# Attention and gated MLP on one core: products of a job under way go ahead of a due batch of values, and unread products behind the jobs that stand in the last layernorm

## The chip, the cores and the metric

The kernel runs on one core of a Trainium2 chip. The metric is the device time of one execution in microseconds (us); lower is better. The engines are TensorE (PE: matmuls; PEld: its weight loads), VectorE (DVE), ScalarE (ACT), GpSimd (POOL) and SyncE (SP, which only issues DMAs here). Each takes its instructions in the order in which the program has them; between engines, semaphores make one wait for another.

## The reference, cut to what matters

One sequence of 2048 rows of 640 values; 32 heads of 20 values each; a gated layer of 1728 columns. All arrays are bfloat16.

```python
def _layernorm(x, axis=-1, eps=1e-5):
    m = jnp.mean(x, axis=axis, keepdims=True)
    v = jnp.var(x, axis=axis, keepdims=True)
    return (x - m) / jnp.sqrt(v + eps)

def _A_ref(x, wqkv, wo):
    q, k, v = ...            # (x @ wqkv), split into 32 heads of 20
    scores = jnp.einsum("bhqd,bhkd->bhqk", q, k) * (Dh ** -0.5)
    p = _softmax(scores, axis=-1)
    o = jnp.einsum("bhqk,bhkd->bhqd", p, v)
    return ... @ wo

def _B_ref(x, w_gate, w_up, w_down):
    g = jnp.einsum("bsd,df->bsf", x, w_gate)
    u = jnp.einsum("bsd,df->bsf", x, w_up)
    return jnp.einsum("bsf,fd->bsd", g * u, w_down)

h = x + _A_ref(_layernorm(x, axis=-1), A_wqkv, A_wo)
h2 = h + _B_ref(_layernorm(h, axis=-1), B_w_gate, B_w_up, B_w_down)
```

## The kernel before, in words

**Scores and exponentials.** The softmax needs one exponential for each of 32 x 2048 x 2048 scores. They are made in 683 *score tiles* of 128 partitions (keys) by 1536 columns (queries). For each tile `emit_S` puts the score products on TensorE (L533; they use 32 of the 128 rows of the array) and one ACTIVATE on ScalarE (L547), which writes a tile E. For some tiles ScalarE does only the first 1024 columns: the last third is computed by VectorE with four instructions (`emit_x` and what follows it, L580 to L591; tiles xv, xt, xe). `x_takes` decides that while the program is written: VectorE must be free in time, and in the last quarter of the queries `room()` must find that the jobs still to do leave enough time.

**Values.** `emit_AV` (L740) multiplies E with the values and adds up in the one PSUM bank acc, in batches of two rounds; these products too are small ones (the rows of four heads side by side). The ones column in the values gives the softmax sums. When a segment (four heads, 512 or 256 queries) is complete, VectorE copies acc (L752).

**Jobs.** All other work of TensorE is cut into jobs that run between score tiles: transposes of normalised rows, projections of q, k and v (L303, L317), and for each quarter of the queries the product with wo (`job_out`, L978), the second layernorm's transposes, the gated layer (`job_glu`, L1065 and L1083: the products with w_up, "wu", and w_gate, "wg", then h = g * u) and the down product (`job_y`, L1129, evacuated by VectorE at L1133, stored by SP at L1139). The weights wu and wg come through two buffers each, or lie in the places of the old queries ("qa"). A job makes one chunk after another; all jobs but few share the one PSUM bank mi, which VectorE has to empty between two chains of products.

**What sets the order.** The Python code is also a planner. It keeps clocks of its own (`at["pe"]`, `at["dve"]`, `at["exp"]`, `at["slot"]`) with assumed durations, and for each score tile i it writes one *slot*, in this order: the score products of tile i and its exponential; then up to two batches of values, if they are due; then finished segments and new jobs; then products of jobs (`run_job`), as many as by the planner's clock end before the next score products have to start; then, if nothing fits, `keep_warm` (L496): a pair of *unread products*, matmuls of ident with kT whose result nobody reads. `cool` lets `emit_S` put a single unread product (L529) ahead of the scores where too few full-array products stood of late. A job that is not at the start of a chain (`cur["fresh"]` is false) has its bank already. The due times in `run_job(until)` come from the next exponential and from the release of the score tile two before.

**The end.** When the last values are through, jobs are taken until none is in the middle of a chain, and `last_tail` does the last 256 queries: out products (L1228, L1230, L1234), with the last softmax sums and their reciprocals between them (L670, L678 to L686, L1243), the second layernorm (bn statistics, then rows normalised half on VectorE, L1257, and half on ScalarE, L1258), then `fill()`, then the transposes of the normalised rows (L283), the gated layer and y. `fill()` does all jobs that are left; at that point these are half tiles of y (14 products each) of the quarter's first 256 queries. By program order they stand between the out products and the transposes.

Behind all this stands a general branch that a flag skips.

Of the kernel before, what the change touches and what calls it, by code (L numbers as in the profile page):

```python
# [61 lines left out]
WO_NS, SUMS_NS, ROOT_NS, ROWS_NS = 1500, 6000, 5000, 5000  # L62
END_OF_TIME = 10 ** 9
WARM_LATE, NEXT_DVE = 0, 300
HOLD_AT, HOLD_NS = 5300, 450
AV_ROUNDS, X_LATE = 2, 0
FULL_IN, FULL_NS, ALL_NS = 2083, 300, 760
# [18 lines left out]
def kernel(  # L86
# [617 lines left out]

    final = {}

    def emit_AV(upto):
        put_x()
        if not av_q:
            return  # L710
        if acc["seg"] is not None and av_q[0][1] != acc["seg"]:
            need_x(acc["seg"])
            put_x()
        s = av_q[0][1]
        p, g, lo, hi, kind = segs[s]
        b, c0, w = PASS[p]
        if acc["seg"] != s:
            if at["pe"] < at["acc"] and now["i"] < acc["from"] and min(u[0] for u in av_q) > now["i"] - E_BUFS:
                return
            acc["seg"], acc["left"], acc["n"] = s, (hi - lo) * HPG, [0] * HPG  # L720
            acc["t"] = accp.tile([P, QB], F32, name="acc")
        most, rows = AV_ROUNDS * HPG * QB // w, [[] for _ in range(HPG)]
        for u in av_q:
            if u[0] > upto or u[1] != s:
                break
            if len(rows[u[3]]) < most // HPG:
                rows[u[3]].append(u)
        ready = sum(len(r) for r in rows)
        if ready < min(most, acc["left"]) and min(u[0] for u in av_q) > upto - E_BUFS + 3:
            return  # L730
        for u in [r[k] for k in range(most // HPG) for r in rows if k < len(r)]:
            av_q.remove(u)
            _, _, kt, j, e = u
            x_used.add((s, kt, j))
            at["pe"] = max(at["pe"], x_ready.get((s, kt, j), 0))
            while x_live and x_live[0] in x_used:
                x_live.popleft()
            ensure(("v", kt, g // (NG // 2)))
            h = HPG * g + j
            nc.tensor.matmul(  # L740
                acc["t"][SLOT * j:SLOT * (j + 1), 0:w],
                lhsT=vx[kt][:, VS * h:VS * h + SLOT], rhs=e,
                start=(acc["n"][j] == 0), stop=(acc["n"][j] == hi - lo - 1))
            acc["n"][j] += 1
        acc["left"] -= ready
        partly.append((at["pe"], ready * w / 9.6))
        at["pe"], at["mode"] = pe_free("A") + -(-ready // HPG) * (w * 5 // 12 + 4), "A"
        if acc["left"] == 0:
            dve(605 if w == QB else 342, 0)
            if kind in ("copy", "only"):  # L750
                asb = parts[g] if kind == "copy" else nrm.tile([P, QB], F32, name="asb")
                nc.vector.tensor_copy(asb[:, 0:w], acc["t"][:, 0:w])  # L752
                if kind == "copy":
                    part[g] = asb
            else:
                asb = part[g]
                nc.vector.tensor_tensor(asb[:, 0:w], acc["t"][:, 0:w], asb[:, 0:w], ALU.add)
            acc["seg"], acc["from"], at["acc"] = None, now["i"] + 2, at["dend"] + DVE_PE
            if s == FINAL:
                final["asb"] = asb  # L760
            elif (p, g) in FAST:
                opens["nf", p, g] = at["dend"] + DVE_PE
                urgent.append((("nf", p, g), job_norm(s, asb)))
            elif kind in ("only", "last"):
                norm(s, asb)
# [448 lines left out]
    def run(gen):  # L1214
        for _ in gen:
            pass

    def last_tail():
        st = tail_st[LAST_B]
        on = On  # L1220
        asb = final["asb"]
        c0 = LAST_T[0] * P
        ps_h = {}

        def out_most(t, hf):
            ps = ps_h[t, hf] = bank()
            cs = slice(hf * HALF, (hf + 1) * HALF)
            nc.tensor.matmul(ps[:, 0:HALF], lhsT=ident[:], rhs=st["xr"][t][:, cs], start=True, stop=False)  # L1228
            for g in range(NG - 1):
                nc.tensor.matmul(ps[:, 0:HALF], lhsT=on[g][:, t * P:(t + 1) * P], rhs=wo[g][:, cs], start=False, stop=False)  # L1230

        def out_last(t):
            for hf in range(2):
                nc.tensor.matmul(ps_h[t, hf][:, 0:HALF], lhsT=on[NG - 1][:, t * P:(t + 1) * P],  # L1234
                                 rhs=wo[NG - 1][:, hf * HALF:(hf + 1) * HALF], start=False, stop=True)
        ta, tb = LAST_T
        out_most(ta, 0)
        bc = sums_to_rows(sums_on_pe(asb, HW), HW)
        out_most(ta, 1)
        ps = rows_to_cols(bc, HW, accp.tile([P, QB], F32, name="acc"))  # L1240
        for k in range(2):
            cs = slice(k * P, (k + 1) * P)
            nc.vector.tensor_tensor(on[NG - 1][:, c0 + k * P:c0 + (k + 1) * P], asb[:, cs], ps[:, cs], ALU.mult)  # L1243
        out_most(tb, 0)
        out_last(ta)
        out_most(tb, 1)
        out_last(tb)
        mv = small.tile([P, 2, 2], F32, name="mv")
        for k, t in enumerate(LAST_T):
            bn(mv, k, None, [ps_h[t, hf][:, 0:HALF] for hf in range(2)])  # L1250
        m32, r = rstd_act(mv, 2)
        mr = small.tile([P, 2], F32, name="mr")
        nc.vector.scalar_tensor_tensor(mr[:], m32[:], -1.0, r[:], ALU.mult, ALU.mult)
        ls = {t: late["s"].tile([P, D], BF16, name="ln2") for t in LAST_T}
        for hf in range(2):
            cs = slice(hf * HALF, (hf + 1) * HALF)
            nc.vector.tensor_scalar(ls[ta][:, cs], ps_h[ta, hf][:, 0:HALF], m32[:, 0:1], r[:, 0:1], ALU.subtract, ALU.mult)  # L1257
            nc.scalar.activation(ls[tb][:, cs], ps_h[tb, hf][:, 0:HALF], ACT.Identity, bias=mr[:, 1:2], scale=r[:, 1:2])  # L1258
        fill()
        run(job_T(ls[ta], st["ln2T"][:, :, ta * P:(ta + 1) * P], "dve", mip.tile([P, D], BF16, name="mi", tag="mi")))  # L1260
        run(job_T(ls[tb], st["ln2T"][:, :, tb * P:(tb + 1) * P], "act", accp.tile([P, QB], F32, name="acc")[:].bitcast(BF16)[:, 0:D]))
        for t in LAST_T:
            for hf in range(2):
                nc.scalar.copy(st["h"][t][:, hf * HALF:(hf + 1) * HALF], ps_h[t, hf][:, 0:HALF])
        st["w", 2] = [w_tile(src, 2, ep.tile([P, EW], BF16, name="E")) for src in (B_w_up, B_w_gate)]
        n_next = 0
        for c in job_glu(st, LAST_T, tuple(range(RES0, FP)) + tuple(range(RES0))):
            n_next += c == NEXT
            if c == NEXT and n_next == 8:
                ok = flag_ok()  # L1270
            if c == NEXT and n_next == 20:
                flag_bad(ok)
        run(job_y(st, LAST_T, True))

    def fill():
        while step() is not None:
            pass
# [32 lines left out]
    while i < n_tiles or av_q:  # L1310
        now["i"] = i
        if i < n_tiles:
            emit_S(i)
        else:
            while step_x():
                pass
        if i == first_last:
            for g in range(NG):
                ensure(("spill", g))
            load_res()  # L1320
        if i == n_tiles:
            root = small.tile([P, 1], BF16, name="root")
            nc.scalar.activation(root[:], ones[:], ACT.Sqrt)
        for _ in range(2):
            emit_AV(i if i >= n_tiles else i - 2 if i >= LAG else i - 3)
            if not av_q or min(u[0] for u in av_q) > i - E_BUFS + 1:
                break
        run_events(i)
        if due:
            rows_early(*due[0][2:])  # L1330
        while due and normed(*due[0][0:2]) and (len(due[0][1]) == NG or normed(str(due[0][2]), range(SPLIT_G))):
            add_tail(*due.pop(0)[2:])
        if i < n_tiles:
            ran = run_job(max(at["exp"] - S_EXP - MARGIN, at["slot"][-2]))
            idle = max(pe_free("F"), at["mi"]) + 2 * 216
            if i > WARM and not ran and cur["fresh"] and idle + SWITCH < max(at["slot"][-2] + WARM_LATE, at["exp"] - S_EXP - MARGIN):
                keep_warm()
                at["pe"], at["mode"] = idle, "F"
            spare(max(pe_free("S"), at["slot"][-2]) + NEXT_DVE)
        i += 1  # L1340
# [103 lines left out]
```

## Time and profile before

| | before |
|---|---|
| median of 3 runs | 916.36 us (915.96 to 916.58) |
| profiled execution, its own time | 916.05 us |
| span of the profiled execution | 914.0 us |
| TensorE busy | 817.5 us (89%) |
| VectorE busy | 702.1 us (77%) |
| ScalarE busy | 866.2 us (95%) |
| GpSimd busy | 57.4 us (6%) |
| DMA | 46.54 MB, mean 51 GB/s |

Rows of the profile name the engine, the line, the operation, the tile written and the tiles read, the shapes and a count. In the groups the two numbers behind the bar are busy time in us and the mean of one instruction in ns, then the idle time of the engine just ahead of them with what ended it. In a timeline the first number is the start in us from the span's start, the second the time that the merged row covers. In the rows of windows each engine has its busy time in us and its instructions, then come the granted TensorE clock (1.00 is full), the share of the DMA engines and GB/s. In the chain of work that ended last each row is a start, a duration, an engine, the tile and the line. In the list of waits the numbers are us in total, times, and the longest.

### The profile page before, as it was taken

What the parts mean: (1) busy time and instruction counts of PE and PEld (TensorE: products, weight loads), DVE (VectorE), ACT (ScalarE), POOL (GpSimd) and SP (SyncE); (2) the same over time, 40 slices, a digit from 0 to 9 for tenths busy, and PEclk for the clock granted to TensorE, in tenths of its full rate; (3) what the DMA queues carried; (4) which work ended last, traced back from release to release, by engine and by line L of the source; (5) the groups of instructions that cost most, each with busy time, mean ns of one, the idle gap of its engine ahead of it and who ended that gap; (6) DMA issues with size and microseconds to landing.
All of it is one profiled execution on the core that took longest, in us unless ns stands there. A gap on an engine that the chain in (4) does not pass through costs nothing.

```text
span 914.0 us, 20094 instructions
## 1 busy us (share of the span) xinstructions
PE 817.5 (89%) x8035; PEld 346.8 (38%) x8115; DVE 702.1 (77%) x1310; ACT 866.2 (95%) x719; POOL 57.4 (6%) x255
## 2 busy tenths in 40 slices
PE   8788999889989899899897888999998999998897
PEld 5233333222223222233232333434434445444575
DVE  8664349899999899899998999798998784542243
ACT  6999999999999999999999999999999999999931
POOL 4210000000001200000003000020001000010000
PEclk9999999999999999999999999999999999999999
DMA  6000011011025022212410022021411211201310
GB/s 195 17 14 1 1 27 27 14 24 37 4 61 149 13 71 72 64 49 90 160 28 14 20 70 68 19 54 49 117 51 42 73 28 51 57 15 50 80 44 18
DMA packets 74203, 46.54 MB, mean 51 GB/s; under 512 B 20380, under 2 KB 70440, under 8 KB 74104
## 3 DMA queue, kind: packets, MB, share of 16 engines
q1 hardware_dynamic: 74104, 45.20, 18.0%
q8 instruction: 65, 1.06, 0.5%
q14 instruction: 34, 0.28, 0.1%
HBM read 37.88 MB, written 7.30 MB: 49 GB/s over the span
## 4 chain that ended last, share of the span: by engine, by line
ACT 67%; issue 17%; PE 10%; DVE 4%; DMA 1%; POOL 1%; SPq 0%; ACTq 0%
ACT E L547 67%; PE sc L533 2%; PE f L1065 2%; PE f L1129 2%; PE acc L740 1%; DVE st L201 1%; PE mi L303 1%; PE mi L978 0%; PE f L1230 0%; PE mi L496 0%; DMA wu<-in_B_w_up_dram 0%; PE mi L317 0%; PE mi L1083 0%; DVE kT L310 0%; DVE vx L270 0%
## 5 line engine op out<-in xcount | busy, mean ns | idle before, releaser
L547 ACT ACTIVATE E<-sc 128x1536 bf16<-128x1536 f32 (+1 forms) x683 | 848.7, 1417 | 6.2 <-PE sc L533 5.9
L533 PE MATMUL sc<-qa,kT 32*128 32x512 bf16 (+1 forms) x1920 | 203.2, 340 | 28.6 <-ACT E L547 16.9
L533 PEld LDWEIGHTS <-kT 32*128 32x128 bf16 x2816 | 84.1, 91 | 244.6 <-issue 206.1
L740 PE MATMUL acc<-E,vx 128*32 128x256 bf16 (+1 forms) x2592 | 170.3, 326 | 1.7 <-DVE vx L270 1.2
L580 DVE TENSOR_SCALAR xv<-sc 128x512 f32<-128x512 f32 x167 | 115.0, 689 | 30.2 <-PE sc L533 26.5
L585 DVE SCALAR_TENSOR_TENSOR xe<-xt,xv 128x512 int16<-128x512 f32 x167 | 113.3, 682 | 1.0
L591 DVE SCALAR_TENSOR_TENSOR xt<-xt,xv 128x512 f32<-128x512 f32 x167 | 112.3, 681 | 0.5
L590 DVE SCALAR_TENSOR_TENSOR xt<-xv 128x512 f32<-128x512 uint16 x167 | 112.0, 683 | 0.3
L303 PE MATMUL mi<-lnT,wp 128*128 128x512 bf16 x279 | 83.3, 381 | 11.7 <-DVE qa L310 5.5
L740 PEld LDWEIGHTS <-vx 128*32 128x32 bf16 x2816 | 55.8, 95 | 66.4 <-issue 63.8
L533 PE MATMUL sc<-qb,kT 32*128 32x256 bf16 (+1 forms) x896 | 68.2, 288 | 8.1 <-ACT E L547 5.3
L1129 PE MATMUL mi<-wd,hh 128*128 128x320 bf16 x336 | 58.2, 301 | 1.6 <-DVE xr L1133 1.6
L740 PE MATMUL acc<-xe,vx 128*32 128x512 bf16 (+1 forms) x224 | 50.6, 332 | 0.0
L1129 PEld LDWEIGHTS <-hh 128*128 128x128 bf16 x448 | 38.7, 97 | 30.6 <-issue 18.7
L303 PEld LDWEIGHTS <-wp 128*128 128x128 bf16 x310 | 25.0, 97 | 55.9 <-issue 44.3
L310 DVE TENSOR_SCALAR kT<-mi,one_row 128x512 bf16<-128x512 f32 x30 | 22.5, 750 | 28.1 <-PE mi L303 24.7
L1065 PE MATMUL mi<-ln2T,wg 128*128 128x512 bf16 x128 | 38.0, 382 | 5.8 <-DVE u L270 5.2
L496 PE MATMUL mi<-kT,ident 128*128 128x512 bf16 x116 | 37.8, 386 | 5.5 <-DVE ln2T L270 1.0
L978 PE MATMUL mi<-wo,on 128*128 128x320 bf16 x224 | 40.5, 301 | 2.2 <-DVE xr L982 2.0
L1065 PE MATMUL mi<-ln2T,wu 128*128 128x512 bf16 x128 | 37.3, 382 | 4.3 <-DVE hh L1073 3.5
L1083 PE MATMUL mi<-ln2T,qa 128*128 128x256 bf16 x240 | 34.6, 274 | 4.1 <-DVE hh L1091 3.0
L207 POOL CAST mb<-mv 128x2 bf16<-128x2 f32 (+1 forms) x10 | 2.3, 231 | 528.6 <-DVE mv L202 410.9
(143 smaller groups left out, 645.0 us busy)
## 6 DMA issues: line engine op xcount, KB each, us to landing
wu<-in_B_w_up_dram SPq DMA_DIRECT2D x23, 320.0 KB
wg<-in_B_w_gate_dram SPq DMA_DIRECT2D x23, 320.0 KB
bc<-scr SPq DMA_DIRECT2D x80, 64.0 KB
qsp<-qa SPq DMA_DIRECT2D x8, 384.0 KB
xr<-in_A_x_dram SPq DMA_DIRECT2D x16, 160.0 KB
bc<-scr SPq DMA_DIRECT2D x76, 32.0 KB
out_dram<-xr SPq DMA_DIRECT2D x14, 160.0 KB
wd<-in_B_w_down_dram SPq DMA_DIRECT2D x13, 160.0 KB
```

The source lines that it names most:

```text
L303: nc.tensor.matmul(ps[:], lhsT=wslice(m, g, c), rhs=lnT[:, c, ch * QB:(ch + 1) * QB], start=(c == 0), stop=(c == KT - 1))
L496: nc.tensor.matmul(ps[:], lhsT=ident[:], rhs=kT[0][:, 0:BANK], start=True, stop=True)
L533: nc.tensor.matmul(sc[:, o:o + w], lhsT=kT[g][SLOT * j:SLOT * (j + 1), kt * P:(kt + 1) * P], rhs=q_of(g, b, c0, w)[SLOT * j:SLOT * (j + 1) ...
L547: exps = nc.scalar.activation(e[:, 0:n_act], sc[:, 0:n_act], ACT.Exp, bias=EXP_BIAS, scale=SM_SCALE)
L580: took = nc.vector.tensor_scalar(v[:], ps, X_SCALE, X_BASE, ALU.mult, ALU.max)
L585: nc.vector.scalar_tensor_tensor(e[:], t[:], X_R, v[:], ALU.mult, ALU.add)
L590: lambda: nc.vector.scalar_tensor_tensor(t[:], u, X_P, u, ALU.add, ALU.mult),
L591: lambda: nc.vector.scalar_tensor_tensor(t[:], t[:], X_Q, u, ALU.add, ALU.mult),
L740: nc.tensor.matmul(acc["t"][SLOT * j:SLOT * (j + 1), 0:w], lhsT=vx[kt][:, VS * h:VS * h + SLOT], rhs=e, start=(acc["n"][j] == 0), stop=(ac ...
L978: nc.tensor.matmul(ps[:, 0:HALF], lhsT=on[g][:, t * P:(t + 1) * P], rhs=wo[g][:, cs], start=(g == 0), stop=(g == NG - 1))
L1065: nc.tensor.matmul(ps[:, 0:n], lhsT=st["w", fp][k][:, c, f_cols(fp, f2)], rhs=st["ln2T"][:, c, c0:c0 + n], start=(c == 0), stop=(c == KT - 1))
L1129: nc.tensor.matmul(ps[:, 0:HALF], lhsT=st["hh"][f // 2][:, f % 2, t * P:(t + 1) * P], rhs=late["Wd"][f][:, cs], start=(f == 0), stop=(f == ...
```

## The change

Two functions are added and called in each slot from tile LAG (10) on, ahead of the values. `av_ns` works out, with the same tests as `emit_AV`, whether a batch of values is due in this slot, and if so how long it takes by the planner's clock. `job_ahead` then lets a job that is in the middle of a chain go on, up to the usual limit less that time. After it the values come, and then `run_job` as before. In a slot with no due batch, or with a job at the start of a chain, nothing changes directly.

In `last_tail`, `fill()` is followed by unread products: as many of 216 ns as fit into what `fill()` leaves, by the planner's clock, of LN_NS = 3300 ns. All other lines are the same; since a planner decides the order, the order of instructions shifts in most of the program.

```diff
+LN_NS = 3300
...
+    def av_ns(upto):
+        if not av_q or acc["seg"] not in (None, av_q[0][1]):
+            return 0
+        s = av_q[0][1]
+        if acc["seg"] is None and at["pe"] < at["acc"] and now["i"] < acc["from"] and min(u[0] for u in av_q) > now["i"] - E_BUFS:
+            return 0
+        w = PASS[segs[s][0]][2]
+        most, rows = AV_ROUNDS * QB // w, [0] * HPG
+        for u in av_q:
+            if u[0] > upto or u[1] != s:
+                break
+            rows[u[3]] = min(rows[u[3]] + 1, most)
+        left = acc["left"] if acc["seg"] == s else END_OF_TIME
+        if sum(rows) < min(most * HPG, left) and min(u[0] for u in av_q) > upto - E_BUFS + 3:
+            return 0
+        return SWITCH + -(-sum(rows) // HPG) * (w * 5 // 12 + 4)
+
+    def job_ahead(upto):
+        ns = av_ns(upto)
+        if not ns:
+            return
+        until = max(at["exp"] - S_EXP - MARGIN, at["slot"][-2]) - ns
+        if not cur["fresh"]:
+            run_job(until)
...
+        begun = at["pe"]
         fill()
+        warm_ps = bank()
+        for _ in range(int((LN_NS - (at["pe"] - begun)) / 216)):
+            nc.tensor.matmul(warm_ps[:], lhsT=ident[:], rhs=kT[0][:, 0:BANK], start=True, stop=True)
         run(job_T(ls[ta], st["ln2T"][:, :, ta * P:(ta + 1) * P], "dve", mip.tile([P, D], BF16, name="mi", tag="mi")))
...
+        if LAG <= i < n_tiles:
+            job_ahead(i - 2)
         for _ in range(2):
             emit_AV(i if i >= n_tiles else i - 2 if i >= LAG else i - 3)
```

## The prediction

> **What bounds the kernel now.** I read first the page's busy shares and the shares of the chain that ended last, then ScalarE's exponentials by shape, and then the same line in four windows.
>
> ```profile
> PE 817.5 (89%) x8035; PEld 346.8 (38%) x8115; DVE 702.1 (77%) x1310; ACT 866.2 (95%) x719; POOL 57.4 (6%) x255
> ...
> ACT 67%; issue 17%; PE 10%; DVE 4%; DMA 1%; POOL 1%; SPq 0%; ACTq 0%
> ```
>
> ```profile
> L547 ACT ACTIVATE E<-sc 128x1536 bf16<-128x1536 f32 x515 | 717.2, 1520 | 5.7 <-PE sc L533 5.5
> L547 ACT ACTIVATE E<-sc 128x1024 bf16<-128x1024 f32 x168 | 178.2, 1100 | 0.5 <-PE sc L533 0.5
> ```
>
> ```profile
> 60.00:350.00 290.00, 289.96 (x234) 1.00 0.13 35
> 350.00:490.00 140.00, 139.78 (x118) 1.00 0.25 75
> 490.00:760.00 270.00, 269.35 (x222) 0.99 0.20 53
> 760.00:870.00 110.00, 109.06 (x83) 1.00 0.17 46
> ```
>
> The 683 exponentials bound the kernel to about 870 us. Between 60 and 870 us ScalarE lacks 0.04 + 0.22 + 0.65 + 0.94 = 1.85 us of 810. There, time falls in two ways only: ScalarE gets less to do, or one of these 1.85 us goes. A tile whose last third goes to VectorE costs ScalarE 1520 - 1100 = 420 ns less.
>
> After 870 us ScalarE is nearly free, and TensorE and a layernorm set the end. The timeline of all engines there, and the last steps of the chain:
>
> ```profile
> 869.95 0.40 PE L740 MATMUL acc<-E,vx 128*32 128x256 bf16 x6 [0.52 <-ACT E L547]
> 870.28 0.31 PE L1228 MATMUL f<-xr,ident 128*128 128x320 bf16 x1
> ...
> 871.38 0.50 PE L670 MATMUL f<-identf,asb 128*128 128x4 f32 x4
> ...
> 875.71 0.43 PE L1234 MATMUL f<-wo,on 128*128 128x320 bf16 x2
> ...
> 875.98 7.83 PE L1129 MATMUL f<-wd,hh 128*128 128x320 bf16 x56
> ...
> 878.28 1.12 DVE L1257 TENSOR_SCALAR ln<-f,m,rstd 128x320 bf16<-128x320 f32 x2
> 878.44 1.13 ACT L1258 ACTIVATE ln<-f,mr,rstd 128x320 bf16<-128x320 f32 x2 [0.48 <-DVE mr L1253]
> 879.32 0.48 DVE L1133 TENSOR_TENSOR xr<-f,xr 128x320 bf16<-128x320 f32 x1
> ...
> 880.51 4.22 SPq L1139 DMA_DIRECT2D out_dram<-xr  x2
> ...
> 883.52 0.68 PEld L283 LDWEIGHTS <-ln 128*128 128x128 bf16 x10
> ```
>
> ```profile
> 876.15 7.67 PE f L1129 x56
> 885.15 11.08 PE f L1065 x100
> 896.32 4.47 PE f L1065 x40
> 900.80 7.70 PE f L1129 x56
> ```
>
> The normalised rows are ready at 878.28 + 1.12 = 879.40 (VectorE's tile) and 878.44 + 1.13 = 879.57 (ScalarE's). Their transposes begin only at 883.52, because 56 down products (four half tiles of y) stand ahead of them on TensorE. The hole is overfilled by 4 us, and all that follows (885.15 to 908.5 in the chain) hangs on it.
>
> **The change part by part.** The two programs' instruction orders show what the diff alone does not, since a planner decides it.
>
> *(1) Products ahead of values.* Slots in which products of a job stand ahead of a batch of values on TensorE go from 3 to 73. Such products wait for no evacuation: the job is under way and its bank open. What they gain is that VectorE empties the bank while the values run. The waits and one late load, on TensorE, SP and ScalarE:
>
> ```profile
> PE sc L533 <- ACT E L547: 22.3, 66, 0.9
> ...
> PE mi L1065 <- DVE u L270: 5.2, 12, 0.7
> PE mi L1083 <- DVE hh L1091: 3.8, 9, 0.5
> ```
>
> ```profile
> 756.23 0.42 SPq L1036 DMA_DIRECT2D wu<-in_B_w_up_dram  x1
> ```
>
> ```profile
> 759.73 1.27 PE L1083 MATMUL mi<-ln2T,wu 128*128 128x256 bf16 x10 [1.03 <-DMA wu<-in_B_w_up_dram]
> ```
>
> ```profile
> 753.75 6.86 ACT L547 ACTIVATE E<-sc 128x1536 bf16<-128x1536 f32 x5
> 761.44 13.71 ACT L547 ACTIVATE E<-sc 128x1536 bf16<-128x1536 f32 x10 [0.84 <-PE sc L533]
> ```
>
> Bank waits such as 5.2 and 3.8 us shrink, but they are off the path: scores wait for ScalarE 22.3 us in all. They count only through what the planner does with the time. It finishes the third quarter's last y at score tile 622 instead of 645, and so finds room for thirds on VectorE: 175 such tiles instead of 168, six of the seven beyond tile 600. ScalarE: 7 x 420 ns = **-2.94 us**. VectorE pays four instructions for each, and has the time:
>
> ```profile
> L580 DVE TENSOR_SCALAR xv<-sc 128x512 f32<-128x512 f32 x167 | 115.0, 689 | 30.2 <-PE sc L533 26.5
> L585 DVE SCALAR_TENSOR_TENSOR xe<-xt,xv 128x512 int16<-128x512 f32 x167 | 113.3, 682 | 1.0
> L591 DVE SCALAR_TENSOR_TENSOR xt<-xt,xv 128x512 f32<-128x512 f32 x167 | 112.3, 681 | 0.5
> L590 DVE SCALAR_TENSOR_TENSOR xt<-xv 128x512 f32<-128x512 uint16 x167 | 112.0, 683 | 0.3
> ```
>
> ```profile
> 760.00:815.00 55.00, 51.39 (x695) 27.74 (x696) 26.18 (x54) 54.16 (x42) 3.60 (x19) 1.00 0.14 36
> ```
>
> Seven times 2.74 us is 19 us; from 760 to 815 us alone VectorE idles 55 - 26.18 = 28.8 us. TensorE is the tight one there, 51.39 of 55. It gets rid of work in that window, because glu and y stand some ten tiles earlier, in slots that had been cut short by a bank.
>
> *(2) The late load.* In the old order the load of wu stands two tiles ahead of its first product; issued at 756.23, it holds TensorE until 759.73 and ScalarE for 0.84 us. In the new order it stands five tiles ahead. With the pitch p of a full exponential from 4p + 1.52 = 6.86, p = 1.335 us, five tiles are 6.7 us against the 3.5 us from issue to use: **-0.84 us**. The price if I am wrong is that 0.84 stays. Elsewhere the lead falls too (second quarter, one pair from 23 tiles to 8), never below five; each load that is late after all costs another 0.84.
>
> *(3) The end of attention.* Three of the four y half tiles now run before the last layernorm. Five products of the third stand ahead of the last values, where TensorE waited 0.52 us. The other nine come behind them and push out-products and sums (L1228 on): 9 x 7.83/56 = **+1.26 us**, as TensorE runs without a pause from 870.28 to the transposes. Its evacuation (0.48 us on VectorE) falls between the copy of the values and the reciprocals, while TensorE does L1228 to L670, 1.1 us: hidden. The store of those rows leaves SP earlier, ahead of the last weights: no cost.
>
> *(4) The hole.* What stands in it is 14 y products and two unread ones: 14 x 0.140 + about 0.43 = 2.4 us, where 876.1 to 879.5 leaves 3.4. So the rows set the time of the transposes: 883.52 - 879.5 = **-4.0 us**. The unread products cost nothing under this cover; without it, 0.43.
>
> *(5) More unread products.* Nine more warming pairs stand in the attention part, and one more single.
>
> ```profile
> 501.45 0.61 PE L496 MATMUL mi<-kT,ident 128*128 128x512 bf16 x2
> ```
>
> 9 x 0.61 = 5.5 us of TensorE if nothing hid them; the planner puts them only where no job fits. Bounds 0 and +5.5; I take 0, since ScalarE's idle row near such pairs (350 to 490 us) shows 0.22 us in 140.
>
> *(6) The clock.* Around the only half-clock stretch ahead of the end:
>
> ```profile
> 501.80:505.00 3.20, 1.83 (x36) 0.70 (x34) 2.67 (x5) 3.20 (x5) 2.16 (x9) 1.00 0.00 0
> 505.00:508.40 3.40, 3.07 (x35) 0.95 (x29) 3.37 (x7) 3.40 (x4) 0.00 (x0) 0.54 0.05 7
> ```
>
> ```profile
> 509.62 10.91 ACT L547 ACTIVATE E<-sc 128x1024 bf16<-128x1024 f32 x9 [0.49 <-PE sc L533]
> ```
>
> After 3.2 us with only scores and values (two slots in a row without a full-array product), TensorE ran 3.4 us at a clock of 0.54, and ScalarE lost 0.49 us behind it. The old order has four such pairs of slots and one tripped; the new has three. Bounds -0.5 and +1.5; I take 0.
>
> Sum: -2.94 - 0.84 + 1.26 - 4.0 = -6.5 us. The profiled execution took 916.05 us (914.0 of span, 2.05 around it); that gives 909.5, and as it lies 0.31 below the median of 916.36, **909.8 us**.
>
> **The rivals.**
>
> *Saved exponentials are lost again.* Scores come later where products go first, or loads with shorter leads come late: three or four such waits of 0.84 us eat (1) and (2). The tight 51.39 of 55 speaks for it, the 22.3 us of waiting scores against. Only the end gains: 916.36 - 2.74 = 913.6.
>
> *Slower: values pushed back make scores late.* In 70 more slots TensorE passes through products and values before the next scores. From 6.5 us / 70 = 93 ns of lateness in each slot the gain is gone; at 150 ns the time is 909.8 + 10.5 = 920. For it: ScalarE has no reserve. Against: the products are cut off at the slot's planned end less the values' own cost, so total work ahead of the scores is bounded as before.
>
> *The hole is too thin and the clock drops.* With 42 products fewer, TensorE is idle for about a microsecond ahead of the transposes. A drop as at 505 would run 3.4 us at half speed on the path: +1.7, so 911.5. By the row at 501.8, where TensorE was busy 1.83 of 3.20 us, it could be; in the hole it is busy 2.4 of 3.4. The Trainium skill, "TensorE: Matmul & The Clock Gate", section "HAM oscillation — how this bites in real kernels", gives as the rule that there be no idle gap above some 3.4 us; by it the hole costs nothing and the sum stays 909.8. The trace agrees on the length of a slow stretch (3.4 us) but not on the need of an idle gap, since TensorE was more than half busy before its drop.
>
> *More than forecast.* Ten exponentials from 761.44 have 9p + 1.52 = 13.71, p = 1.354, 19 ns above the best. If the earlier evacuations gave back a quarter of that on 508 tiles, 2.4 us: 907.4.
>
> That nothing is moved is excluded by the order.
>
> **How the numbers follow.** Forecast 0.60 (908.3 to 911.2); savings lost again 0.17 (912.5 to 914.5, with 0.03 of it above 914.5); thin hole 0.05; more than forecast 0.08; slower 0.10, 0.02 of it ending in no change. 0.2% is 1.8 us, about what a measurement can tell: 914.5 to 918.2 is the same. Faster 0.60 + 0.14 + 0.05 + 0.08 = 0.87, same 0.05, slower 0.08. The range takes in (5)'s and (6)'s smaller bounds and the second case: 907.3 to 914.3.
>
> **What would show it.** ScalarE's groups: 508 and 175 exponentials; no 0.84 us ahead of one near 760 us. Idle of L547 from 60 us on below 2 us: (1) arrived; at 4 to 5, the first rival; above 8, the slower one. Last exponential ending some 3.8 us earlier. Between the last L1234 product and the transposes 3.4 us instead of 7.4, with a gap on TensorE after the unread products. Nine y products between the last values and the first out-product. The windows' clock at 1.00 there. Wrong would make me a new half-clock stretch, or scores that come late all over.

## The result, and the profile after

| | before | after |
|---|---|---|
| median | 916.43 us (9 runs, 915.96 to 918.36) | 918.88 us (9 runs, 917.76 to 920.3) |
| profiled execution, its own time | 916.05 us | 920.3 us |
| its span | 914.0 us | 918.3 us |
| end of the last exponential | 869.90 us | 876.65 us |
| from there to the end of VectorE's last evacuation | 39.12 us | 36.04 us |
| behind it, to the end of the span | 5.0 us | 5.6 us |

The ratio of the times is 1.0023, with a 95% interval of 1.0013 to 1.0034. The changed kernel is slower by 0.23%, some 2.1 us (2.45 us by the medians); forecast were 909.8 us, and 907.3 to 914.3 as the range. The prediction was wrong in its sign. The profiled execution is the slowest of the nine, 1.4 us above their median; about that much of it is a half-clock stretch at 44.5 us, which an execution of e1 (below), with the same order on TensorE, VectorE and ScalarE, does not have.

The page's busy shares and chain, ScalarE's exponentials by shape, and the same line in windows, of the kernel after (L548 is the old L547; the lines from `emit_AV` on lie 26 further down):

```profile
PE 829.8 (90%) x8055; PEld 345.5 (38%) x8136; DVE 719.7 (78%) x1338; ACT 864.8 (94%) x719; POOL 58.1 (6%) x255
...
ACT 54%; PE 20%; issue 14%; DVE 8%; DMA 2%; POOL 1%; SPq 0%; ACTq 0%; DVEq 0%
```

```profile
L548 ACT ACTIVATE E<-sc 128x1536 bf16<-128x1536 f32 x508 | 708.0, 1512 | 9.3 <-PE sc L534 7.3 <-PE acc L766 1.2 <-PE mi L1155 0.2
L548 ACT ACTIVATE E<-sc 128x1024 bf16<-128x1024 f32 x175 | 184.3, 1088 | 4.9 <-PE sc L534 4.9
```

```profile
60.00:350.00 290.00, 283.08 (x227) 0.98 0.13 34
350.00:490.00 140.00, 139.87 (x119) 1.00 0.25 75
490.00:760.00 270.00, 268.32 (x220) 1.00 0.21 54
760.00:876.70 116.70, 116.42 (x91) 1.00 0.17 45
```

508 and 175 exponentials are there, as forecast. But ScalarE now lacks 6.92 + 0.13 + 1.68 + 0.28 = 9.01 us between 60 us and its last exponential, where it lacked 1.85, and 6.92 of them lie between 60 and 350 us. The engines' timelines around the largest gap, one for each engine, SP first:

```profile
263.60 0.38 SPq L1062 DMA_DIRECT2D wu<-in_B_w_up_dram  x1
...
265.73 8.86 SPq L982 DMA_DIRECT2D wd<-in_B_w_down_dram  x14
274.69 0.51 SPq L637 DMA_DIRECT2D sums<-asb  x1
277.92 0.33 SPq L638 DMA_DIRECT2D sums_all<-sums  x1
```

```profile
267.99 0.69 DVE L778 COPY asb<-acc 128x512 f32<-128x512 f32 x1
```

```profile
279.54 0.25 DVE L648 RECIPROCAL ri<-sums_all 128x16 f32<-128x16 f32 x1 [3.25 <-DMA sums_all<-sums]
280.26 0.48 DVE L1008 TENSOR_TENSOR xr<-mi,xr 128x320 bf16<-128x320 f32 x1
...
280.79 2.29 PE L1004 MATMUL mi<-wo,on 128*128 128x320 bf16 x8 [2.64 <-DVE xr L1008]
...
283.72 1.02 ACT L548 ACTIVATE E<-sc 128x1024 bf16<-128x1024 f32 x1 [3.68 <-PE sc L534]
```

It is one sequence. A finished segment's softmax sums were copied at 267.99 + 0.69 = 268.68, and their way through DRAM (stored at L637, read back spread over partitions at L638, reciprocals at L648) begins on SP. SP was then issuing the weight loads of the second quarter, four for wu and wg and 14 for the down product ("wd", 13 of 160 KB and one of 80); the store left only at 274.69, 6.0 us after the copy. The reciprocal waited on VectorE for 3.25 us. Behind it in VectorE's order stood L1008, which empties the bank mi; TensorE waited 2.64 us for that bank with the scores behind it in its own order; ScalarE then lacked 3.68 us.

The same queue of the kernel before has the two the other way round: sums first, burst of weights behind them.

```profile
266.81 0.50 SPq L636 DMA_DIRECT2D sums<-asb  x1
268.50 0.34 SPq L637 DMA_DIRECT2D sums_all<-sums  x1
...
273.35 9.22 SPq L956 DMA_DIRECT2D wd<-in_B_w_down_dram  x14
```

There is a second loss in the same place. The store took 274.69 to 277.92 = 3.23 us until its readers could follow, where before it took 268.50 - 266.81 = 1.69. In windows of SP, with the share of the DMA engines and the GB/s last:

```profile
270.00:274.60 4.60, 1.00 1.01 331
274.69:277.90 3.21, 1.00 0.52 167
```

In the 3.21 us the DMA engines still moved 167 GB/s, 0.54 MB, for a store of 8 KB: the loads were still draining. The Trainium skill, "DMA: Bandwidth & Descriptors", section "Queues, rings and completion order", says that what one issuing engine sends goes through one ring on each DMA engine and is consumed in ring order. The trace agrees as far as it goes: the store landed 1.5 us later than behind a quiet queue.

Third, the clock fell behind the starved stretch. Windows of all engines (PE, PEld, DVE, ACT, POOL, then the clock):

```profile
276.40:279.80 3.40, 1.75 (x18) 0.51 (x16) 0.26 (x2) 3.40 (x4) 0.00 (x0) 1.00 0.08 14
279.80:286.60 6.80, 5.81 (x29) 1.80 (x28) 5.53 (x10) 2.60 (x3) 0.00 (x0) 0.52 0.19 40
```

The windows begin some 0.2 us early; the granted clock was 0.50 from 280.04 to 286.87.

The end went as forecast. TensorE in the last layernorm, kernel after:

```profile
876.70 0.40 PE L766 MATMUL acc<-E,vx 128*32 128x256 bf16 x6 [0.47 <-ACT E L548]
877.02 1.40 PE L1155 MATMUL mi<-wd,hh 128*128 128x320 bf16 x9
878.26 0.30 PE L1254 MATMUL f<-xr,ident 128*128 128x320 bf16 x1
...
883.68 0.43 PE L1260 MATMUL f<-wo,on 128*128 128x320 bf16 x2
...
883.95 2.06 PE L1155 MATMUL f<-wd,hh 128*128 128x320 bf16 x14
885.85 0.38 PE L1289 MATMUL f<-kT,ident 128*128 128x512 bf16 x1
...
886.90 0.28 PE L284 MATMUL mi<-ident,ln 128*128 128x128 bf16 x2 [0.67 <-DVE ln L1283]
...
888.82 4.42 PE L1091 MATMUL f<-ln2T,qa 128*128 128x256 bf16 x39 [0.78 <-ACT ln2T L268]
```

Nine y products stand ahead of the out-products: the first of these starts 878.26 - 876.70 = 1.56 us after the start of the last values, where it was 870.28 - 869.95 = 0.33. Unread products close the hole (L1289; the program has two, the trace a record of one), and the transposes wait only for the rows. From the last wo products to the first product of the gated layer it is 888.82 - 883.68 = 5.14 us, where it was 885.15 - 875.71 = 9.44: 4.30 less. From the last exponential to the last evacuation the kernel is 39.12 - 36.04 = 3.08 us shorter. What follows, the last store above all, takes between 5.0 and 5.9 us over the profiled executions of all the kernels here, in executions of the same end too (5.0 before, 5.5 in e5).

For the account of what follows I add up the distances from the start of one exponential to that of the next, less 1330 ns for each of 1536 columns and 904 for each of 1024. These floors are mine, near the best pitch of the trace. The 168 and 175 short ones make the floors 835.9 and 832.9 us, 3.0 less; the excess over the floors is 17.31 us before and 26.93 after, 9.6 more. Of this 6.9 lies in tiles 200 to 250 (0.90 and 7.79), and 1.4 in the stretch at 44.5 us.

### The profile page after: what moved, and what is told of

Read it like the earlier page. It is cut to its first block, busy times and chain, and to the rows that moved or that the text cites. A ratio compares the mean times of both kernels' runs of the same rounds, so it can differ in the third digit from the quotient of the medians.

```text
span 918.3 us, 20172 instructions
## 1 busy us (share of the span) xinstructions
PE 829.8 (90%) x8055; PEld 345.5 (38%) x8136; DVE 719.7 (78%) x1338; ACT 864.8 (94%) x719; POOL 58.1 (6%) x255
## 4 chain that ended last, share of the span: by engine, by line
ACT 54%; PE 20%; issue 14%; DVE 8%; DMA 2%; POOL 1%; SPq 0%; ACTq 0%; DVEq 0%
ACT E L548 54%; PE sc L534 5%; PE acc L766 3%; PE mi L1109 2%; PE mi L1091 2%; PE f L1091 2%; PE mi L1004 1%; DVE st L202 1%; DVE xv L581 1%; PE mi L304 1%; DMA wd<-in_B_w_down_dram 1%; PE f L1155 1%; PE mi L1155 1%; PE mi L497 1%; DVE xt L591 1%
## 5 line engine op out<-in xcount | busy, mean ns | idle before, releaser
L548 ACT ACTIVATE E<-sc 128x1536 bf16<-128x1536 f32 (+1 forms) x683 | 847.3, 1403 | 14.3 <-PE sc L534 12.2
L534 PEld LDWEIGHTS <-kT 32*128 32x128 bf16 x2816 | 81.6, 91 | 246.3 <-issue 210.8
L581 DVE TENSOR_SCALAR xv<-sc 128x512 f32<-128x512 f32 x174 | 119.9, 689 | 33.1 <-PE sc L534 30.1
L586 DVE SCALAR_TENSOR_TENSOR xe<-xt,xv 128x512 int16<-128x512 f32 x174 | 117.9, 681 | 0.9
L592 DVE SCALAR_TENSOR_TENSOR xt<-xt,xv 128x512 f32<-128x512 f32 x174 | 117.0, 680 | 0.3
L591 DVE SCALAR_TENSOR_TENSOR xt<-xv 128x512 f32<-128x512 uint16 x174 | 116.8, 683 | 0.3
L1155 PE MATMUL mi<-wd,hh 128*128 128x320 bf16 x378 | 65.9, 301 | 2.1 <-DVE xr L1159 2.1
L766 PE MATMUL acc<-xe,vx 128*32 128x256 bf16 (+1 forms) x237 | 55.9, 329 | 0.0
L497 PE MATMUL mi<-kT,ident 128*128 128x512 bf16 x133 | 42.8, 384 | 7.7 <-DVE u L271 2.4
```

The source lines that it names most:

```text
L497: nc.tensor.matmul(ps[:], lhsT=ident[:], rhs=kT[0][:, 0:BANK], start=True, stop=True)
L534: nc.tensor.matmul(sc[:, o:o + w], lhsT=kT[g][SLOT * j:SLOT * (j + 1), kt * P:(kt + 1) * P], rhs=q_of(g, b, c0, w)[SLOT * j:SLOT * (j + 1) ...
L548: exps = nc.scalar.activation(e[:, 0:n_act], sc[:, 0:n_act], ACT.Exp, bias=EXP_BIAS, scale=SM_SCALE)
L581: took = nc.vector.tensor_scalar(v[:], ps, X_SCALE, X_BASE, ALU.mult, ALU.max)
L586: nc.vector.scalar_tensor_tensor(e[:], t[:], X_R, v[:], ALU.mult, ALU.add)
L591: lambda: nc.vector.scalar_tensor_tensor(t[:], u, X_P, u, ALU.add, ALU.mult),
```

## The experiments

**e1_wd_apart: the changed kernel, the 14 loads of wd issued one for every two slots.** The order on the other three engines stays that of the changed kernel. If the store behind the burst is the cause, this undoes it and leaves all products where they are; e5 below asks what the parting is worth by itself.

```diff
+    def wd_later():
+        for f in range(2 * FP):
+            later(16 + 2 * f, lambda f=f: load_wd([f]))
...
-                load_wd()
+                wd_later()
```

> The changed kernel with the 14 loads of the down weights put off on SP in three groups behind the stores of the softmax sums; the order on TensorE, VectorE and ScalarE is exactly that of the changed kernel. Theory A (the burst of loads stands ahead of the sums' store on SP, the reciprocal on VectorE waits 3.25 us for it, and the products and scores behind it stand still): the 3.68 us of ScalarE at 283 us and the stops up to 330 us go, some 6 us, so about 912.5 us, which is faster than before. Rival B (products ahead of values make scores late, the loads are innocent): within 1 us of the changed kernel, about 918.5. Rival C (TensorE's clock drops because full-array products stand differently): ScalarE still loses several us around 280 to 330 us, about 917.

Measured: 913.9 us (12 runs, 913.64 to 919.45), a ratio of 0.9981 (0.9968 to 0.9995) to the kernel before: by the medians 5.0 us less than the changed kernel, by the ratios 3.9, and less than before. SP's timeline:

```profile
267.38 0.51 SPq L637 DMA_DIRECT2D sums<-asb  x1
269.08 0.34 SPq L638 DMA_DIRECT2D sums_all<-sums  x1
...
278.84 2.32 SPq L982 DMA_DIRECT2D wd<-in_B_w_down_dram  x5
```

The sums leave at once and land in 1.70 us; the 14 loads come in three groups (5, 3 and 6), each behind the sums of a segment. The excess of tiles 200 to 250 falls from 7.79 to 2.90. The burst on SP is the main cause.

**e5_before_wd_apart: the same parting in the kernel before.**

> The kernel before with the same parting of the down-weight loads as in the first run. In the trace of before no engine waits for a sums' landing there, so theory A says 916.4, within 0.7 us; a gain of 2 us or more would say that the parting is worth something by itself, and that the first run cannot be read as an undoing.

Measured: 916.58 us (11 runs), ratio 1.0002 (0.9992 to 1.0011). Where the sums stand ahead of the burst, parting it is worth nothing. e1's gain belongs to the changed order.

**e2_before_wd_late: the kernel before, its burst put later and made 19 loads long, so that a store of sums would fall behind it.**

```diff
+    def wd_late():
+        load_wd()
+        load_wd(range(5))
...
-                load_wd()
+                later(16, wd_late)
```

> The kernel before, its order on TensorE, VectorE and ScalarE untouched; only the burst of down-weight loads comes later on SP, behind the broadcasts of the segment then under way, with five of the loads made twice, so that some 13 us of issuing stand ahead of the next sums' store (293.25 us in the trace of before). Theory A: the reciprocal, at 299.8 before, waits some 5 us, ScalarE loses 4 to 7 us, 920 to 923 us. Rivals B and C: no product is moved, so 916.4.

Measured: 916.27 us (11 runs), ratio 0.9999 (0.999 to 1.0008). The experiment missed its aim, as SP's timeline shows:

```profile
280.34 9.25 SPq L956 DMA_DIRECT2D wd<-in_B_w_down_dram  x19
293.22 0.51 SPq L636 DMA_DIRECT2D sums<-asb  x1
```

The 19 loads were through 3.6 us before the store came. It only tells that a longer and later burst with nothing behind it is free.

**f2_before_wd_hit: the same with 37 loads, long enough to meet that store.**

```diff
+    def wd_late():
+        load_wd()
+        load_wd()
+        load_wd(range(9))
```

> The first attempt put 19 loads ahead of the sums' store, but their issue ended at 289.6 us, before the store at 293.2, so nothing met. Now 37 loads (the 14 down weights twice, nine of them three times) stand there in the kernel before, some 18 us of issuing from 280 us on, to 298; orders on TensorE, VectorE and ScalarE untouched. Theory A (the position ahead of a sums' store is the cause): the reciprocal, due at 299.8, waits 3 us or more, ScalarE loses 2 to 5 us behind it, 918.5 to 921.5. If a late reciprocal is hidden in this place, 916.4 and the stall needs more than the late store.

Measured: 924.29 us (5 runs, 922.96 to 925.13), ratio 1.0084 (1.0071 to 1.0097), 7.7 us slower. SP, then VectorE, TensorE and ScalarE:

```profile
279.93 19.17 SPq L956 DMA_DIRECT2D wd<-in_B_w_down_dram  x37
299.54 0.53 SPq L636 DMA_DIRECT2D sums<-asb  x1
302.43 0.33 SPq L637 DMA_DIRECT2D sums_all<-sums  x1
```

```profile
304.15 0.25 DVE L647 RECIPROCAL ri<-sums_all 128x16 f32<-128x16 f32 x1 [4.35 <-DMA sums_all<-sums]
...
306.75 0.71 PE L283 MATMUL mi<-ident,ln 128*128 128x128 bf16 x5 [4.05 <-DVE ln L243]
...
308.12 1.45 ACT L547 ACTIVATE E<-sc 128x1536 bf16<-128x1536 f32 x1 [4.03 <-PE sc L533]
```

The mechanism made by hand in a kernel that does not have it, and it has the same parts: store 6.3 us later than in e2, 2.89 us to land, a reciprocal that holds VectorE, TensorE and then ScalarE idle, and the clock at 0.50 from 303.4 to 310.2. One link differs: behind the reciprocal stand here the rows that VectorE normalises (L243), and TensorE's transposes wait for these 4.05 us, not for the bank. By the excess of tiles 200 to 250 (6.07 against 0.90) this place costs 5.2 us; the rest of the 7.7 lies elsewhere. Together with e1 and e5 this shows the mechanism from both sides.

**f5_two_steps: e1, and GpSimd's root in the layernorms left with one Newton step fewer.** e1 still has 20.65 - 17.31 = 3.3 us more excess than before. Its list of waits has a candidate; the rows of before, e1 and f5:

```profile
DVE rstd L238 <- POOL den L232: 2.0, 2, 1.1
```

```profile
DVE rstd L239 <- POOL den L233: 6.2, 4, 3.4
```

```profile
DVE rstd L241 <- POOL den L235: 2.5, 2, 2.3
```

The second layernorm's roots run on GpSimd, and VectorE's reciprocal takes them. In the new order the jobs reach it sooner.

```diff
+            if ve_ is nc.gpsimd and k == 2:
+                break
```

> The first run's kernel with the last of the three refinement steps of the root left out on GpSimd (four small instructions for each of eight groups of rows); the order on all other engines is the same. Theory D (what the first run still loses against the kernel before, 3.3 us of ScalarE, is in part VectorE standing still for the late root, 1.6 us at 306 us and 3.4 us at 510 us in its trace): these waits shrink by 0.8 us or more each, ScalarE loses 1 us less, about 912.9. Rival: the waits are covered, 913.9.

Measured: 911.47 us (5 runs, 910.56 to 913.02), ratio 0.9944 (0.9931 to 0.9957), 2.4 us below e1's median, 3.4 by the ratios. The excess falls to 18.04. In windows of the exponentials of f5 ScalarE lacks 0.67 + 0.13 + 0.87 + 0.23 = 1.90 us from 60 us on, as good as the 1.85 of before:

```profile
60.00:350.00 290.00, 289.33 (x233) 1.00 0.13 34
350.00:490.00 140.00, 139.87 (x118) 1.00 0.25 77
490.00:760.00 270.00, 269.13 (x222) 1.00 0.20 53
760.00:867.20 107.20, 106.97 (x83) 1.00 0.18 48
```

**g1_before_two: the same step left out of the kernel before.**

> The kernel before with the last refinement step of the root left out on GpSimd; order on the other engines as before. In its trace VectorE waits 2.0 us for late roots, against 6.2 in the changed one. Theory D (the changed order reaches the second layernorm's rows earlier and so meets the late root): here the step is worth 1 us at most, 915.5 to 916.5. If it is worth 2.4 us as in the changed order, about 914.2, the late root is a fault of both.

Measured: 915.22 us (10 runs, 914.13 to 918.09), ratio 0.9977 (0.9968 to 0.9986), 1.7 us below before (2.1 by the ratio), more than the 1 us that I had allowed. So the late root is a fault of both kernels: by the medians only 2.4 - 1.7 = 0.7 us of f5's step is due to the change, by the ratios 3.4 - 2.1 = 1.3, by the excess of the traces up to 20.65 - 18.04 = 2.6. How the step divides stays open between these; g1's own profiled execution had a clock drop near 57 us, so its excess can't decide it.

**e4_before_short_fill: the kernel before without the 56 y products in the hole** (256 rows of the output are not computed).

```diff
-        fill()
+        held.clear(), jobs.clear()
+        cur["gen"] = None
```

> The kernel before without the four half tiles of y in the last layernorm's hole (56 products left out, so 256 rows of the output are not written). If the rows normalised at 879.5 set the time of the transposes as forecast, the end comes 4.0 us sooner: 912.4. If the empty hole of 3.4 us lets the clock drop to half, 1.7 us of it are lost again: 914.1.

Measured: 915.26 us (11 runs, 913.48 to 918.24), ratio 0.9987 (0.9976 to 0.9998), 1.3 us less than before. The end of its profiled execution, up to the last evacuation, is 3.03 us shorter, not 4.0, and the clock fell to half from 880.8 to 884.2, behind the empty hole. So in this execution an empty hole gave part of its gain back through the clock. The whole execution is only 1.4 us shorter, since 0.9 of the gain is missing behind the last evacuation and 0.8 ahead of and among the exponentials; that is not explained.

**f4_no_unread: e1 without the unread products in the hole** (`LN_NS = 0`).

> The first run's kernel (loads parted) without the two unread products in the last layernorm's hole. The rows set the time of the transposes, so the products only matter if the clock drops without them: 913.9 if not, up to 1.7 us more if it does.

Measured: 915.15 us (11 runs, 913.68 to 917.87), ratio 0.9984 (0.9974 to 0.9994), 1.25 us above e1's median. By the ratios alone the two are not told apart; by the trace the end is 37.64 us instead of 36.04. The windows of f4:

```profile
878.00:882.20 4.20, 2.67 (x23) 1.71 (x22) 3.54 (x12) 1.70 (x4) 0.00 (x0) 1.00 0.00 0
882.20:885.60 3.40, 3.03 (x15) 2.15 (x15) 0.42 (x1) 2.01 (x6) 0.00 (x0) 0.54 0.84 237
```

Without two products of about 0.2 us each the clock halved in this execution for 3.4 us on the path, to 0.50 from 882.47. The step shows in the trace; in the medians it is not clear of noise.

**f3_before_room: the kernel before, with VectorE taking more thirds** (`ROOM = 0`, 174 short exponentials instead of 168). It has the prediction's first term without the new order.

> The kernel before with ROOM 0 in place of 5000, so that the planner gives six more thirds to VectorE in the last quarter, and no products go ahead of values. If a third is worth its 420 ns wherever scores keep up, 916.4 - 2.5 = 913.9. If the last quarter is bound by TensorE once ScalarE has less to do, the saving is lost again as late scores: 916 or more.

Measured: 917.19 us (12 runs, 914.5 to 919.12), ratio 1.0001 (0.9991 to 1.0012). Its exponentials end 2.57 us earlier, at 867.33, but TensorE's work did not get ahead with them, and ten products of the gated layer stand behind the last values:

```profile
867.38 0.40 PE L740 MATMUL acc<-E,vx 128*32 128x256 bf16 x6 [0.52 <-ACT E L547]
867.71 1.27 PE L1083 MATMUL mi<-ln2T,qa 128*128 128x256 bf16 x10
```

The end is 1.09 us longer (40.21 against 39.12). By the trace 1.5 us should be left; the medians show none of it, and the spread of these runs is as wide as that. So the thirds alone, without jobs that have gone ahead, did not pay here.

**g2_nine_in_hole: f5, and the nine y products left for the hole**, where they take the place of the unread ones.

```diff
-    while ("loadB",) not in done or not cur["fresh"]:
+    while ("loadB",) not in done:
```

> The kernel of the fourth run of the second set (loads parted, two refinement steps), in which the half tile of y under way when attention ends is finished in the last layernorm's hole and not ahead of the out products; 9 and 14 products then stand in the hole, no unread ones. If the nine cost 1.26 us where they were, as forecast, about 910.2. If they were covered there, 911.5 as before.

Measured: 910.29 us (6 runs, 909.73 to 911.32), ratio 0.9927 (0.9914 to 0.994), the best of all, 6.7 us below before; its interval overlaps that of f5. In its timeline of TensorE the hole is full of work that somebody reads:

```profile
874.33 1.39 PE L1161 MATMUL mi<-wd,hh 128*128 128x320 bf16 x9
875.55 2.06 PE L1161 MATMUL f<-wd,hh 128*128 128x320 bf16 x14
...
878.20 0.44 PE L286 MATMUL mi<-ident,ln 128*128 128x128 bf16 x5 [0.58 <-DVE xr L1165]
```

The end is 35.32 us against 36.04: 0.72 of the 1.26 us of part (3) come back. The rest is a new wait of 0.58 us, as the transposes need the bank that VectorE empties of y (L1165) only behind the normalised rows.

## Why the prediction was wrong, step by step

*(1) Products ahead of values: right in its count.* 508 and 175 exponentials, and so 3.0 us less of floor against the 2.94 forecast; the floors are my constants and no measurement. In f5, where both faults below are taken away, the stretch from the start of the first exponential to the end of the last is 852.0 us against 854.3, 2.3 less, where (1) and (2) together were forecast at 3.78. "They count only through what the planner does with the time" was only half of it: the planner also sent the weight loads of the second quarter's jobs to SP earlier (the first of wd at 265.73 us against 273.35).

*(2) The late load: the step that failed.* The 0.84 us at 760 us went as forecast. But "Elsewhere the lead falls too (second quarter, one pair from 23 tiles to 8), never below five; each load that is late after all costs another 0.84" asks only whether a load comes in time for its own product. No load came late: in the list of waits after, no product waits for a weight load. What came late was the store of the softmax sums, which the same loads push back on SP. By e1 that cost 5.0 us (medians) or 3.9 (ratios), about twice the whole distance between the two kernels. The prediction counts stores and reciprocals only at the end of attention; those of the segments, and what a late one would cost, are nowhere in it, although SP's order gave them: sums ahead of the burst in one program, behind it in the other.

*(3) The end of attention: right.* Nine products, 1.56 - 0.33 = 1.23 us against 1.26. g2 shows that they were not forced there.

*(4) The hole: right in size, wrong in one sentence.* -4.30 us against -4.0; (3) and (4) together were forecast at -2.74 and gave -3.08. "The unread products cost nothing under this cover" is true, but I also gave them no worth, and by f4's trace they carry 1.6 us of it (1.25 by the medians, not clear of noise). The rival of a thin hole had the right mechanism and price (1.7 us), and in the traces the unread products kept it away.

*(5) More unread products: right.* ScalarE lacks 0.13 us from 350 to 490 us.

*(6) The clock: in its place a follower.* The drop at 505 us is gone; in the changed kernel there are others, 6.8 us from 280.0 behind the late sums, then one at 310.8 and one at 44.5. e1, f5 and g2 have none before the end. As the page "TensorE: Matmul & The Clock Gate" of the Trainium skill has it (section "HAM oscillation — how this bites in real kernels"), the rule is that there be no idle gap above some 3.4 us. By f4 that is not enough: TensorE was busy for 1.61 of the 3.41 us right ahead of its drop, and its longest wait there was 0.89 us.

*The rivals.* "Above 8" us of idle was my sign for values that push scores back in every slot. 9.01 came, but the mechanism is another: the loss is not spread over 70 slots at 93 ns. Most of it sits in one place, and f5 runs the 73 slots with 1.90 us of idle. The slower case had the right sign for the wrong reason. *More than forecast* did not come: the excess is 18.04 in f5 against 17.31 before, so on balance ScalarE got nothing back.

*A second, smaller fault.* The late roots belong to no part of the prediction either: a chain on GpSimd for which VectorE waited 2.0 us in all before and 6.2 after.

*What stays open.* With both faults taken away f5 stands at 911.47, 1.7 us above the forecast. The floors (-3.0), the end (-3.08) and 0.7 us more excess make -5.4 against the forecast -6.5; the excess has new single stalls at tiles 240 (0.89 us, scores late) and 411 (0.79), whose causes I did not try to undo.

## What to carry to other kernels

A step that lets work go earlier also lets its loads go earlier. For each issuing queue, list what now stands behind those loads and who waits for that: here an 8 KB store, behind 2.2 MB of weights that e1 could load 16 to 42 slots later, cost 3.9 to 5.0 us, more than the 1.7 to 2.7 us by which e1 beats the kernel before. And an in-order engine that evacuates the one bank of all jobs can pass on its waits for a DMA or for GpSimd; put short results ahead of long loads, and part a burst that has slack.

## What I had not expected of the hardware

Two unread products of 512 columns in a gap, about half a microsecond of TensorE's time, can decide on its clock: it stayed at 1.00 there in the traced executions that have them (after, e1, f5) and fell to half in the one without them (f4), which cost 1.6 us by the traces. Each is one execution, and the medians do not tell e1 and f4 apart.

A drop needs no long pause. In the 3.41 us right ahead of it TensorE was busy for 1.52 us (280.04 in the kernel after), 1.61 (f4) and 2.04 (505.29 before, mostly with scores and values); e1, with the unread products in the same place, was busy for 2.09 of 3.41 and kept its clock. No threshold comes out of these figures. All slow stretches ahead of the last product are 3.41 or 6.83 us long. The Trainium skill ("TensorE: Matmul & The Clock Gate", section "What's actually happening") gives a window of 3413 ns. The traces agree with it. As one drop came at 44.5 us in one execution and not in another of the same order, single executions of one kernel can differ by a microsecond or more, so differences of this size are read here from medians of several executions.
